# Products accumulated on a copied PSUM bank in the block scheme of two MLPs

## The chip, the core and the metric

One NeuronCore of a Trainium2 chip runs the whole program. TensorE (PE) multiplies and writes its sums to PSUM, which has eight banks of 128 partitions x 512 fp32 numbers here; ScalarE (ACT) and VectorE (DVE) read PSUM and SBUF; GpSimd (POOL) does little; SyncE (SP) issues the DMAs. The metric is the device time of the program in microseconds.

## What is computed

```
kv  = einsum(softmax(k over the sequence), v)        # 8 batches x 8 heads, 576 x 64
x   = softmax(q over the head's 64) @ kv             # joined to x [4608, 512]
h   = x @ moe_w_in;  g = h * sigmoid(1.702 h)        # [4608, 2048], layer 0
x   = g @ moe_w_out                                  # [4608, 512]
h   = x @ moe2_w_in; g = max(0.01 h, h)              # layer 1
out = g @ moe2_w_out
```

All in fp32. Every number that goes into a product is split into a high and a low half (`split_hi`, a cast on ScalarE; `split_lo`, a subtraction on VectorE), and every product is three matmul terms: high x high, low weight x high, high weight x low.

## The kernel before

The 4608 tokens are nine chunks of 512, which are columns of a matmul; the 512 features are four blocks of 128. Chunks 0 to 7 are taken in pairs (c, c + 1). A "pass" is one pair in one layer, written (layer, c): (0,0), (0,2), (0,4), (0,6), (1,0), (1,2), (1,4), (1,6), and chunk 8 apart. The attention of later chunks runs in the gaps of the layer-0 passes, step by step (maxima `kma`/`kmb`, exponentials, `kvp`, `kv` at L492, transposes `qtp`, the product `pxt` at L556).

The first matmul of a pair takes two blocks of the hidden dimension (columns f0, f1) and two chunks at a time, a "quad", with a scheme of seven block products in place of eight. Each product is six matmuls 128 x 512 (`product`, L732). A pass has eight quads. The seven products go to three PSUM banks, a, b and c (`ha`, `hb`, `hc`): the first to a, the second to b, the third to c, and then four more are accumulated on a, b, c, b. With p1 the first product, the four results are

- a after its second product,
- v5 = b (second product) + c's first + p1,
- u2 = b's first + p1 + c with its second product,
- p1 + b after its third product.

So the first product is copied to SBUF by ScalarE (L905), and VectorE makes five additions (the `add` at L900), each of which reads one bank and one tile of SBUF. The results go to the activation: `act1` (ScalarE, Tanh or Prelu) and in layer 0 `act2` (VectorE). In `quad_step` (passes (0,2), (0,4), (0,6), (1,0): 32 quads) the second matmul (`acc`, L789, 24 matmuls a quad) runs between the products. In `quad_apart` (passes (1,2), (1,4), (1,6): 24 quads) it doesn't; there `pair_apart` makes the second matmul behind it with the same seven-product scheme, in seven rounds of 24 matmuls on bank pairs a, c, a, b, b, c, b, and writes the results out through transposes (`out_part`: `otp`, then ScalarE's copy `ev`, then a store).

In layer 0, weights of layer 1 are prepared at the same time: raw blocks are loaded (`raw`), converted by ScalarE (L109, L112) and VectorE (L116 to L130), and stored again (`w`, `o`). PSUM is full: four banks `acc0` to `acc3`, three banks `h` (a, b, c) and one for the attention and the transposes.

What stands where on an engine is decided by a scheduler that goes through the program by priority; the code's own order and its `gaps` lists say where pieces of other work are offered. An engine then runs its instructions strictly in that order.

Of the kernel before, what the change touches and what calls it, by code (L numbers as in the profile page):

```python
# [26 lines left out]
def tile_softmax_linear_attention_two_mlps(  # L27
# [721 lines left out]
    def act1(layer, h, t):  # L749
        if layer == 0:  # L750
            nc.scalar.activation(t, h, AF.Tanh, scale=0.851)
        else:
            nc.scalar.activation(t, h, AF.Prelu, alpha=0.01)  # L753
# [135 lines left out]
    def run(items):  # L889
        for fn in items:  # L890
            fn()


    def quad_step(layer, n, gaps, extra):


        tiles = quad.pop((layer, n))
        W = {name: tiles[m][:, b, :, :] for name, (m, b) in OPS.items()}
        f0, f1 = 2 * n, 2 * n + 1
        add = lambda out, h, t: nc.vector.tensor_tensor(out=out, in0=h, in1=t, op=ALU.add)  # L900
        run(gaps[0])
        a = ps.tile([P, T], F32, tag="h", name="ha", bufs=3)
        product(a, "a11", W["w11"], True)
        p1 = pool["cv"].tile([P, T], F32, tag="p1", name="p1", bufs=2)
        nc.scalar.copy(p1, a)  # L905
        run(gaps[1])
        b = ps.tile([P, T], F32, tag="h", name="hb", bufs=3)
        product(b, "s2", W["t2"], True)
        u2 = pool["cv"].tile([P, T], F32, tag="u2", name="u2", bufs=2)
        add(u2, b, p1)  # L910
        run(gaps[2])
        c = ps.tile([P, T], F32, tag="h", name="hc", bufs=3)
        product(c, "s1", W["t1"], True)
        v5 = pool["cv"].tile([P, T], F32, tag="v5", name="v5", bufs=2)
        add(v5, c, p1)
        run(gaps[3])
        product(a, "a12", W["w21"], False)
        t11 = new_g(1, f0)
        act1(layer, a, t11)
        act2(layer, a, t11)  # L920
        halve_hi(f0, t11)
        run(gaps[4])
        product(b, "s3", W["t3"], False)
        add(v5, b, v5)
        halve_lo(f0)
        t22 = new_g(2, f1)
        act1(layer, v5, t22)
        act2(layer, v5, t22)
        run(gaps[5])
        product(c, "s4", W["w22"], False)  # L930
        add(u2, c, u2)
        run(gaps[6])
        t12 = new_g(1, f1)
        act1(layer, u2, t12)
        act2(layer, u2, t12)
        halve_hi(f1, t12)
        run(extra[0:1])
        halve_lo(f1)
        run(gaps[7])
        product(b, "a22", W["t4"], False)  # L940
        add(p1, b, p1)
        t21 = new_g(2, f0)
        act1(layer, p1, t21)
        run(gaps[8])
        act2(layer, p1, t21)
        run(extra[1:2])
        run(gaps[9])

# [2 lines left out]
    def quad_apart(layer, n, gaps):  # L951


        tiles = quad.pop((layer, n))
        W = {name: tiles[m][:, b, :, :] for name, (m, b) in OPS.items()}
        add = lambda out, h, t: nc.vector.tensor_tensor(out=out, in0=h, in1=t, op=ALU.add)  # L956
        m, o = divmod(n, 2)
        if o == 0:
            for name in ("a11", "a12", "a21", "a22"):
                G[name, m] = pool["g"].tile([P, 2, T], F32, tag=name, name=name, bufs=4)  # L960
        t11, t12, t21, t22 = (G[name, m][:, o, :] for name in ("a11", "a12", "a21", "a22"))
        run(gaps[0])
        a = ps.tile([P, T], F32, tag="h", name="ha", bufs=3)
        product(a, "a11", W["w11"], True)
        nc.scalar.copy(t21, a)
        run(gaps[1])
        b = ps.tile([P, T], F32, tag="h", name="hb", bufs=3)
        product(b, "s2", W["t2"], True)
        add(t12, b, t21)
        run(gaps[2])  # L970
        c = ps.tile([P, T], F32, tag="h", name="hc", bufs=3)
        product(c, "s1", W["t1"], True)
        add(t22, c, t21)
        run(gaps[3])
        product(a, "a12", W["w21"], False)
        act1(layer, a, t11)
        run(gaps[4])
        product(b, "s3", W["t3"], False)
        add(t22, b, t22)
        act1(layer, t22, t22)  # L980
        run(gaps[5])
        product(c, "s4", W["w22"], False)
        add(t12, c, t12)
        act1(layer, t12, t12)
        run(gaps[6])
        run(gaps[7])
        product(b, "a22", W["t4"], False)
        add(t21, b, t21)
        act1(layer, t21, t21)
        run(gaps[8])  # L990
        if o == 1:
            y = G["a21", m]
            nc.vector.tensor_tensor(out=y, in0=y, in1=G["a22", m], op=ALU.add)
        run(gaps[9])
# [15 lines left out]
    def pair_apart(c, steps, fetched):  # L1010


        add = lambda out, h, t: nc.vector.tensor_tensor(out=out, in0=h, in1=t, op=ALU.add)
        pages = [(r, m) for r in range(len(ROUNDS)) for m in range(NQ // 2)]
        halves_of = {}

        def prepare(k):
            r, m = pages[k]
            src = G[ROUNDS[r][1], m]
            hl = new_halves()  # L1020
            split_hi(src, hl[0])
            split_lo(src, *hl)
            halves_of[k] = hl
            if r == 0:
                sub(src, G["a21", m], src)
            elif r == 1:
                sub(src, G["a22", m], G["a11", m])
            elif r == 2:
                sub(src, src, G["a11", m])

        def acc2(n):
            tags = dict(a=("acc0", "acc1"), b=("acc2", "acc3"), c=("h", "h"))[n]
            return [ps.tile([P, T], F32, tag=t, name=f"o{n}", bufs=3 if t == "h" else 1) for t in tags]

        def tmp(tag):
            return [pool["cv"].tile([P, T], F32, tag=tag, name=tag, bufs=2) for _ in range(2)]

        banks = {}
        prepare(0)
        for k, (r, m) in enumerate(pages):  # L1040
            while len(fetched) < min(k + 4, len(pages)):
                rr, mm = pages[len(fetched)]
                fetched.append(load_round(ROUNDS[rr][0], mm))
            if k + 1 < len(pages):
                prepare(k + 1)
            run(steps.get(k, ()))
            name = "acabbcb"[r]
            if m == 0 and r in (0, 1, 3):
                banks[name] = acc2(name)
            w, (gh, gl) = fetched[k], halves_of.pop(k)  # L1050
            for l in range(2):
                for d in range(2):
                    sl = slice(d * P, (d + 1) * P)
                    for i, (wh, x) in enumerate(((0, gh), (1, gh), (0, gl))):
                        first_one = r in (0, 1, 3) and m == 0 and l == 0 and i == 0
                        nc.tensor.matmul(  # L1056
                            banks[name][d], w[:, l, wh, sl], x[:, l, :],
                            start=first_one, stop=(m == NQ // 2 - 1 and l == 1 and i == 2),
                            skip_group_check=(r not in (0, 1, 3)),
                        )  # L1060
            if m < NQ // 2 - 1:
                continue
            h = banks[name]
            for d in range(2):
                if r == 0:
                    if d == 0:
                        p1 = tmp("p1")
                    nc.scalar.copy(p1[d], h[d])
                elif r == 1:
                    if d == 0:  # L1070
                        v5 = tmp("v5")
                    add(v5[d], h[d], p1[d])
                elif r == 3:
                    if d == 0:
                        u2 = tmp("u2")
                    add(u2[d], h[d], p1[d])
                elif r == 2:
                    t = pool["cv"].tile([P, T], F32, tag="ev", name="ev", bufs=4)
                    nc.scalar.copy(t, h[d])
                    out_part(c, d, t)  # L1080
                elif r == 4:
                    add(v5[d], h[d], v5[d])
                    out_part(c + 1, 2 + d, v5[d])
                elif r == 5:
                    add(u2[d], h[d], u2[d])
                    out_part(c, 2 + d, u2[d])
                else:
                    add(p1[d], h[d], p1[d])
                    out_part(c + 1, d, p1[d])

    def pair_first(layer, c, units, held, work):

# [315 lines left out]

    ready(0)
    held = pair_second(0, 1, second_steps(units, (0, 2)))  # L1410
    for i, (layer, c) in enumerate(order):
        nxt = order[i + 1] if i + 1 < len(order) else None
        if split and c < LAST:
# [97 lines left out]
```

## Time and profile before

| | |
|---|---|
| median of 3 runs | 1627.37 us (1627.02 to 1627.89) |
| the profiled execution, whole | 1628.65 us |
| its span in the profile | 1626.9 us |
| PE busy | 1587.7 us, 98% |
| VectorE / ScalarE busy | 1053.7 / 800.9 us, 65% / 49% |
| granted TensorE clock, mean | 0.997 |

The profile is one execution. A timeline row gives the start, the duration, the engine and its line, output and input, and in brackets how long the engine stood idle before and what ended that. Matmuls in a row overlap, so the last one's duration reaches a little past the start of the next group. "PEld" is PE loading weights. The chain of waits is followed back from the last instruction to what released each step.

### The profile page before, as it was taken

What the parts mean: (1) busy time and instruction counts of PE and PEld (TensorE: products, weight loads), DVE (VectorE), ACT (ScalarE), POOL (GpSimd) and SP (SyncE); (2) the same over time, 40 slices, a digit from 0 to 9 for tenths busy, and PEclk for the clock granted to TensorE, in tenths of its full rate; (3) what the DMA queues carried; (4) which work ended last, traced back from release to release, by engine and by line L of the source; (5) the groups of instructions that cost most, each with busy time, mean ns of one, the idle gap of its engine ahead of it and who ended that gap; (6) DMA issues with size and microseconds to landing.
All of it is one profiled execution on the core that took longest, in us unless ns stands there. A gap on an engine that the chain in (4) does not pass through costs nothing.

```text
span 1626.9 us, 22121 instructions
## 1 busy us (share of the span) xinstructions
PE 1587.7 (98%) x7632; PEld 1268.3 (78%) x7632; DVE 1053.7 (65%) x1623; ACT 800.9 (49%) x1698; POOL 35.2 (2%) x162
## 2 busy tenths in 40 slices
PE   5999999999999999999999999999999999999998
PEld 3677778777877778778888888788888888888887
DVE  7899659786776757667544666644774487547411
ACT  7787656556545655445333545333453354334422
POOL 1000000000000002000000000000000000000000
PEclk9999999999999999999999999999999999999999
DMA  8788577778788887978896977996776777676763
GB/s 215 226 274 256 167 234 269 255 247 262 249 281 264 260 260 243 303 253 281 306 330 228 321 272 264 316 292 203 242 209 203 233 212 215 194 230 195 223 192 102
DMA packets 221775, 397.84 MB, mean 245 GB/s; under 512 B 57568, under 2 KB 138464, under 8 KB 221664
## 3 DMA queue, kind: packets, MB, share of 16 engines
q1 hardware_dynamic: 221664, 396.43, 76.1%
q8 instruction: 61, 1.00, 0.3%
q14 instruction: 50, 0.41, 0.1%
HBM read 306.18 MB, written 90.18 MB: 244 GB/s over the span
## 4 chain that ended last, share of the span: by engine, by line
PE 77%; DVE 7%; DMA 7%; issue 3%; ACT 1%; SPq 1%; ACTq 0%; DVEq 0%; POOL 0%; POOLq 0%
PE acc L789 23%; PE hb L732 13%; PE ha L732 9%; PE hc L732 8%; PE h L719 7%; PE ob L1056 6%; PE oa L1056 4%; PE oc L1056 4%; DMA o<-cv 2%; PE pxt L556 2%; DMA wo<-wp 1%; DMA w<-cv 1%; DVE cv L126 1%; DVE gl L86 1%; DMA raw<-in_moe_w_in_dram 1%
## 5 line engine op out<-in xcount | busy, mean ns | idle before, releaser
L789 PE MATMUL acc<-gh,wo 128*128 128x512 f32 x1152 | 362.8, 396 | 2.6 <-ACT wo L83 1.8
L789 PEld LDWEIGHTS acc<-gh,wo 128*128 128x128 f32 x1152 | 211.5, 188 | 48.9 <-ACT wo L83 2.2
L789 PE MATMUL acc<-gl,wo 128*128 128x512 f32 x576 | 225.6, 392 | 0.0
L719 PE MATMUL h<-x,wi 128*128 128x512 f32 x768 | 191.3, 399 | 2.8 <-ACT wi L83 2.8
L719 PEld LDWEIGHTS h<-x,wi 128*128 128x128 f32 x768 | 144.2, 191 | 37.2 <-ACT wi L83 4.4
L732 PE MATMUL ha<-x,wa 128*128 128x512 f32 x624 | 161.8, 393 | 2.8 <-ACT p L905 2.8
L732 PEld LDWEIGHTS ha<-x,wa 128*128 128x128 f32 x624 | 115.6, 188 | 33.0 <-issue 5.7
L83 ACT CAST sh<-a 128x1024 fp32r<-128x1024 f32 x84 | 88.2, 1050 | 94.4 <-PE oc L1056 35.1
L86 DVE TENSOR_TENSOR sl<-a,sh 128x1024 fp32r<-128x1024 f32 x84 | 102.7, 1222 | 49.4 <-ACT sh L83 49.0
L789 PEld LDWEIGHTS acc<-gl,wo 128*128 128x128 f32 x576 | 108.3, 188 | 23.8 <-issue 0.8
L956 DVE TENSOR_TENSOR a<-hb,a 128x512 f32<-128x512 f32 x72 | 49.7, 690 | 91.3 <-PE hb L732 91.3
L732 PE MATMUL hb<-x,wc 128*128 128x512 f32 x384 | 97.4, 389 | 0.0
L508 ACT ACTIVATE qt<-qt,qmx 128x64 f32<-128x64 f32 x256 | 86.0, 338 | 13.0 <-DVE qmx L498 12.2
L1056 PE MATMUL ob<-sh,wo 128*128 128x512 f32 x288 | 91.7, 394 | 0.0
L732 PE MATMUL hb<-xb,wb 128*128 128x512 f32 x336 | 86.1, 390 | 0.0
L83 ACT CAST gh<-gb 128x512 fp32r<-128x512 f32 x80 | 49.3, 617 | 71.8 <-PE acc L789 69.6
L732 PEld LDWEIGHTS hb<-x,wc 128*128 128x128 f32 x384 | 72.1, 188 | 14.9
L789 PE MATMUL acc<-wo,gh 128*128 128x512 f32 x256 | 79.2, 390 | 1.3 <-DMA wo<-wp 1.3
L83 ACT CAST gh<-gf 128x512 fp32r<-128x512 f32 x96 | 59.1, 616 | 42.5 <-DVE gf L757 33.6
L86 DVE TENSOR_TENSOR gl<-gb,gh 128x512 fp32r<-128x512 f32 x80 | 54.7, 687 | 35.5 <-ACT gh L83 34.2
L86 DVE TENSOR_TENSOR gl<-gf,gh 128x512 fp32r<-128x512 f32 x96 | 65.9, 687 | 18.0 <-ACT gh L83 17.1
L753 ACT ACTIVATE a<-a 128x512 f32<-128x512 f32 x72 | 45.5, 632 | 64.2 <-DVE a L956 64.2
(182 smaller groups left out, 2842.2 us busy)
## 6 DMA issues: line engine op xcount, KB each, us to landing
wo<-wo SPq DMA_DIRECT2D x144, 512.0 KB, 4.6
wo<-wp SPq DMA_DIRECT2D x68, 512.0 KB, 3.6
wo<-wt SPq DMA_DIRECT2D x48, 512.0 KB, 3.6
wa<-wq SPq DMA_DIRECT2D x40, 512.0 KB, 4.0
wb<-wq SPq DMA_DIRECT2D x40, 512.0 KB, 4.2
wc<-wq SPq DMA_DIRECT2D x40, 512.0 KB, 4.7
raw<-in_moe_w_in_dram SPq DMA_DIRECT2D x32, 512.0 KB, 4.9
raw<-in_moe_w_out_dram SPq DMA_DIRECT2D x32, 512.0 KB, 4.9
```

Of the source, the lines that this page charges most:

```text
L83: nc.scalar.copy(hi, src)
L86: nc.vector.tensor_tensor(out=lo, in0=src, in1=hi.bitcast(F32), op=ALU.subtract)
L126: nc.vector.scalar_tensor_tensor(out=w[:, o], in0=hw, scalar=0xC0000000, in1=w[:, o], op0=ALU.bitwise_and, op1=ALU.bitwise_or)
L508: nc.scalar.activation(t[:, h, r, :], t[:, h, r, :], AF.Exp, bias=mx[:, h, r : r + 1], accum_out=sm[:, h, r : r + 1],)
L556: nc.tensor.matmul(pv[o, :, a:e], kvb[b, j][o, :], t[o, :, a:e], start=True, stop=True)
L719: nc.tensor.matmul(h, WI[f][:, b, wh, o * P : (o + 1) * P], xs[f"a{side}{b + 1}"][xh][:, o, :], start=(i == 0), stop=(i == n - 1),)
L732: nc.tensor.matmul(h, w[:, wh, o * P : (o + 1) * P], xo[xh][:, o, :], start=(start and i == 0), stop=(i == 5), skip_group_check=not start,)
L753: nc.scalar.activation(t, h, AF.Prelu, alpha=0.01)
L789: nc.tensor.matmul(acc[d], lhsT, rhs, start=(f == 0 and i == 0), stop=(f == NF - 1 and i == 2))
L956: add = lambda out, h, t: nc.vector.tensor_tensor(out=out, in0=h, in1=t, op=ALU.add)
L1056: nc.tensor.matmul(banks[name][d], w[:, l, wh, sl], x[:, l, :], start=first_one, stop=(m == NQ // 2 - 1 and l == 1 and i == 2), skip_group ...
```

## The change

The first product's bank is no longer copied to SBUF but by ScalarE into the second bank, b. The products come in the order a, c, b, and b's product is accumulated upon the copy, so that p1 is inside bank b from then on. u2 and v5 start as ScalarE copies of b and c; two VectorE additions stay (v5 += b, u2 += c). The last result is bank b itself, which the activation reads from PSUM. The same is done in `quad_apart` and, with bank pairs, in `pair_apart`, where the last round's result is copied by ScalarE in place of an addition. Before the first quad three matmuls `hp` write the three `h` banks once. A quad has three ScalarE copies in place of one and two VectorE additions in place of five.

```diff
@@ quad_step
-        a = ps.tile([P, T], F32, tag="h", name="ha", bufs=3)
+        a, b, c = (ps.tile([P, T], F32, tag="h", name=f"h{x}", bufs=3) for x in "abc")
         product(a, "a11", W["w11"], True)
-        p1 = pool["cv"].tile([P, T], F32, tag="p1", name="p1", bufs=2)
-        nc.scalar.copy(p1, a)
+        nc.scalar.copy(b, a)
         run(gaps[1])
-        b = ps.tile([P, T], F32, tag="h", name="hb", bufs=3)
-        product(b, "s2", W["t2"], True)
-        u2 = pool["cv"].tile([P, T], F32, tag="u2", name="u2", bufs=2)
-        add(u2, b, p1)
-        run(gaps[2])
-        c = ps.tile([P, T], F32, tag="h", name="hc", bufs=3)
         product(c, "s1", W["t1"], True)
         v5 = pool["cv"].tile([P, T], F32, tag="v5", name="v5", bufs=2)
-        add(v5, c, p1)
+        nc.scalar.copy(v5, c)
+        run(gaps[2])
+        product(b, "s2", W["t2"], False)
+        u2 = pool["cv"].tile([P, T], F32, tag="u2", name="u2", bufs=2)
+        nc.scalar.copy(u2, b)
         run(gaps[3])
...
         product(b, "a22", W["t4"], False)
-        add(p1, b, p1)
         t21 = new_g(2, f0)
-        act1(layer, p1, t21)
+        act1(layer, b, t21)
         run(gaps[8])
-        act2(layer, p1, t21)
+        act2(layer, b, t21)
@@ quad_apart
         product(a, "a11", W["w11"], True)
-        nc.scalar.copy(t21, a)
+        nc.scalar.copy(b, a)
         run(gaps[1])
-        b = ps.tile([P, T], F32, tag="h", name="hb", bufs=3)
-        product(b, "s2", W["t2"], True)
-        add(t12, b, t21)
+        product(c, "s1", W["t1"], True)
+        nc.scalar.copy(t22, c)
         run(gaps[2])
-        c = ps.tile([P, T], F32, tag="h", name="hc", bufs=3)
-        product(c, "s1", W["t1"], True)
-        add(t22, c, t21)
+        product(b, "s2", W["t2"], False)
+        nc.scalar.copy(t12, b)
...
         product(b, "a22", W["t4"], False)
-        add(t21, b, t21)
-        act1(layer, t21, t21)
+        act1(layer, b, t21)
@@ pair_apart
             h = banks[name]
+            if r == 0:
+                banks["b"] = acc2("b")
+            elif r == 1:
+                v5 = tmp("v5")
+            elif r == 3:
+                u2 = tmp("u2")
             for d in range(2):
                 if r == 0:
-                    if d == 0:
-                        p1 = tmp("p1")
-                    nc.scalar.copy(p1[d], h[d])
+                    nc.scalar.copy(banks["b"][d], h[d])
                 elif r == 1:
-                    if d == 0:
-                        v5 = tmp("v5")
-                    add(v5[d], h[d], p1[d])
+                    nc.scalar.copy(v5[d], h[d])
                 elif r == 3:
-                    if d == 0:
-                        u2 = tmp("u2")
-                    add(u2[d], h[d], p1[d])
...
+                    nc.scalar.copy(u2[d], h[d])
...
                 else:
-                    add(p1[d], h[d], p1[d])
-                    out_part(c + 1, d, p1[d])
+                    t = pool["cv"].tile([P, T], F32, tag="ev", name="ev", bufs=4)
+                    nc.scalar.copy(t, h[d])
+                    out_part(c if r == 2 else c + 1, d, t)
@@ before the first quad
+    hi = XO["a11"][0]
+    for i in range(3):
+        h = ps.tile([P, T], F32, tag="h", name="hp", bufs=3)
+        nc.tensor.matmul(h, hi[:, 0, 0:P], hi[:, 0, :], start=True, stop=True)
```

The scheduler puts the instructions in another order. On ScalarE, at the head of the second quad of pass (0,4), before (`cv<-raw` are the two conversions, `gb<-p` the Tanh of the last quad's fourth result, `p<-ha` the copy of the first product):

```order
L83 CAST gh<-gf 128x512
L109 ACTIVATE cv_4790<-raw_4755 128x512
L112 ACTIVATE cv_4790<-raw_4755 128x512
L751 ACTIVATE gb<-p_4766 128x512
L905 COPY p_4911<-ha 128x512
L751 ACTIVATE gf<-ha 128x512
```

After, at the same place (`gb<-hb` is that Tanh, `hb<-ha` the copy into bank b, `v` and `u` the copies of c and b):

```order
L83 CAST gh<-gf 128x512
L751 ACTIVATE gb<-hb 128x512
L109 ACTIVATE cv_4779<-raw_4745 128x512
L112 ACTIVATE cv_4779<-raw_4745 128x512
L904 COPY hb<-ha 128x512
L908 COPY v_4915<-hc 128x512
L912 COPY u_4929<-hb 128x512
L751 ACTIVATE gf<-ha 128x512
```

The Tanh has moved ahead of the two conversions, and the copy stands right behind them.

On ScalarE, at the attention step of (0,4) around 545 us, before (L508 are the exponentials of q, `kv` the scaling of kvp, L587 the copy out of pxt):

```order
L751 ACTIVATE gf<-u_5305 128x512
L83 CAST gh<-gf 128x512
L109 ACTIVATE cv_5512<-raw_5377 128x512
L112 ACTIVATE cv_5512<-raw_5377 128x512
L751 ACTIVATE gb<-p_5289 128x512
L508 ACTIVATE qt,qsm<-qt,qmx 128x64
L492 ACTIVATE kv_5423<-kvp,krs 128x64
L508 ACTIVATE qt,qsm<-qt,qmx 128x64 x7
L587 COPY xr<-pxt 128x512
L905 COPY p_5479<-ha 128x512
```

After:

```order
L751 ACTIVATE gf<-u_5303 128x512
L83 CAST gh<-gf 128x512
L112 ACTIVATE cv_5493<-raw_5360 128x512
L751 ACTIVATE gb<-hb 128x512
L492 ACTIVATE kv_5405<-kvp,krs 128x64
L508 ACTIVATE qt,qsm<-qt,qmx 128x64 x6
L587 COPY xr<-pxt 128x512
L508 ACTIVATE qt,qsm<-qt,qmx 128x64 x2
L904 COPY hb<-ha 128x512
L908 COPY v_5477<-hc 128x512
L912 COPY u_5491<-hb 128x512
L109 ACTIVATE cv_5493<-raw_5360 128x512
```

The first conversion (L109) has moved from ahead of `kv` to behind the next quad's three copies; one exponential fewer stands ahead of `kv`.

On PE, at the end of the first pair's second matmul, before (`otp` are the four transposes of one page):

```order
L1056 MATMUL ob<-sl,wo 128x512
L732 MATMUL ha<-x,wa 128x512
L1004 MATMUL otp<-ident,p_10884 128x128 x4
L732 MATMUL ha<-x,wa 128x512 x3
L732 MATMUL hb<-xb,wb 128x512
L1004 MATMUL otp<-ident,p_10885 128x128 x4
L732 MATMUL hb<-xb,wb 128x512 x5
L732 MATMUL hc<-x,wb 128x512 x6
```

After:

```order
L1049 MATMUL ob<-sl,wo 128x512
L732 MATMUL ha<-x,wa 128x512
L997 MATMUL otp<-ident,ev 128x128 x4
L732 MATMUL ha<-x,wa 128x512
L732 MATMUL hc<-x,wb 128x512
L997 MATMUL otp<-ident,ev 128x128 x4
L732 MATMUL hc<-x,wb 128x512 x5
L732 MATMUL hb<-xb,wb 128x512 x6
```

Between the two groups of transposes stand two matmuls in place of four, and the product on c is ahead of that on b.

## Rows read from the trace of the kernel before

**Rows 1.** The page's parts 0 and 1: span, and busy time of each engine.

```profile
span 1626.9 us, 22121 instructions
...
PE 1587.7 (98%) x7632; PEld 1268.3 (78%) x7632; DVE 1053.7 (65%) x1623; ACT 800.9 (49%) x1698; POOL 35.2 (2%) x162
```

**Rows 2.** PE waits after 250 us: line, releaser: total us, times, longest.

```profile
PE pxt L556 <- ACT kv L492: 2.9, 3, 1.2
PE ha L732 <- ACT p L905: 2.8, 2, 2.4
...
PE hb L732 <- DVE u L900: 0.8, 1, 0.8
...
PE kmb L456 <- DVE km L451: 0.3, 1, 0.3
```

**Rows 3.** Chain that ended last, in pass (1,0): start, us, what.

```profile
917.82 2.72 PE acc L789 x12
...
932.78 2.72 PE acc L789 x12
```

**Rows 4.** Groups by form: count, busy us, mean ns, idle before.

```profile
L956 DVE TENSOR_TENSOR a<-hb,a 128x512 f32<-128x512 f32 x72 | 49.7, 690 | 91.3 <-PE hb L732 91.3
...
L900 DVE TENSOR_TENSOR p<-hb,p 128x512 f32<-128x512 f32 x32 | 21.9, 683 | 0.5 <-PE hb L732 0.5
...
L905 ACT COPY p<-ha 128x512 f32<-128x512 f32 x32 | 18.6, 581 | 12.3 <-PE ha L732 12.1
...
L965 ACT COPY a<-ha 128x512 f32<-128x512 f32 x24 | 14.1, 587 | 0.3
```

**Rows 5.** Timeline, a quad of pass (1,0): start, us, engine, line, idle before.

```profile
924.45 1.52 PE L732 MATMUL ha<-x,wa 128*128 128x512 f32 x6
...
926.01 0.59 ACT L905 COPY p<-ha 128x512 f32<-128x512 f32 x1 [0.74 <-PE ha L732]
...
927.17 1.52 PE L732 MATMUL hc<-xb,wb 128*128 128x512 f32 x6
...
929.89 1.52 PE L732 MATMUL hb<-x,wc 128*128 128x512 f32 x6
```

**Rows 6.** Timeline, head of the second quad of (0,4).

```profile
458.50 1.62 PE L732 MATMUL hc<-x,wb 128*128 128x512 f32 x6
...
460.85 0.65 ACT L112 ACTIVATE cv<-raw 128x512 f32<-128x512 f32 x1
...
462.54 1.66 PE L732 MATMUL ha<-x,wa 128*128 128x512 f32 x6 [2.42 <-ACT p L905]
...
466.39 1.53 PE L732 MATMUL hc<-xb,wd 128*128 128x512 f32 x6
```

**Rows 7.** Timeline, head of the second quad of (0,6).

```profile
652.03 1.22 PEld L732 LDWEIGHTS hc<-x,wb 128*128 128x128 f32 x6 [0.42 <-DVE p L900]
...
652.38 0.65 ACT L112 ACTIVATE cv<-raw 128x512 f32<-128x512 f32 x1
...
658.03 1.30 PE L732 MATMUL hc<-xb,wd 128*128 128x512 f32 x5
```

**Rows 8.** Timeline, one attention step inside (0,4).

```profile
545.52 0.67 ACT L109 ACTIVATE cv<-raw 128x512 uint32<-128x512 uint32 x1 [2.62 <-DMA wd<-wq]
...
550.75 1.08 PE L556 MATMUL pxt<-qT,kv 64*64 64x448 f32 x8 [1.19 <-ACT kv L492]
...
551.77 1.66 PE L732 MATMUL ha<-x,wa 128*128 128x512 f32 x6
...
554.39 0.57 ACT L905 COPY p<-ha 128x512 f32<-128x512 f32 x1
```

**Rows 9.** Timeline, end of the first pair's second matmul.

```profile
1221.01 1.37 DVE L1013 TENSOR_TENSOR p<-ob,p 128x512 f32<-128x512 f32 x2 [2.68 <-PE ob L1056]
...
1222.45 0.59 ACT L1006 COPY ev<-otp 128x512 f32<-128x512 f32 x1 [5.38 <-PE otp L1004]
...
1223.09 0.46 PEld L1004 LDWEIGHTS otp<-ident,p 128*128 128x128 f32 x4 [0.18 <-ACT ev L1006]
```

More of the change, by code (lines that the diff above doesn't have):

```diff
@@ L962, in quad_apart @@
         run(gaps[0])
-        a = ps.tile([P, T], F32, tag="h", name="ha", bufs=3)
+        a, b, c = (ps.tile([P, T], F32, tag="h", name=f"h{x}", bufs=3) for x in "abc")
         product(a, "a11", W["w11"], True)
-        nc.scalar.copy(t21, a)
+        nc.scalar.copy(b, a)
         run(gaps[1])
-        b = ps.tile([P, T], F32, tag="h", name="hb", bufs=3)
-        product(b, "s2", W["t2"], True)
-        add(t12, b, t21)
+        product(c, "s1", W["t1"], True)
+        nc.scalar.copy(t22, c)
         run(gaps[2])
-        c = ps.tile([P, T], F32, tag="h", name="hc", bufs=3)
-        product(c, "s1", W["t1"], True)
-        add(t22, c, t21)
+        product(b, "s2", W["t2"], False)
+        nc.scalar.copy(t12, b)
         run(gaps[3])
@@ L1047, in pair_apart @@
             name = "acabbcb"[r]
-            if m == 0 and r in (0, 1, 3):
+            if m == 0 and r < 2:
                 banks[name] = acc2(name)
@@ L1054, in pair_apart @@
                     for i, (wh, x) in enumerate(((0, gh), (1, gh), (0, gl))):
-                        first_one = r in (0, 1, 3) and m == 0 and l == 0 and i == 0
+                        first_one = r < 2 and m == 0 and l == 0 and i == 0
                         nc.tensor.matmul(
@@ L1058, in pair_apart @@
                             start=first_one, stop=(m == NQ // 2 - 1 and l == 1 and i == 2),
-                            skip_group_check=(r not in (0, 1, 3)),
+                            skip_group_check=(r >= 2),
                         )
@@ L1063, in pair_apart @@
             h = banks[name]
+            if r == 0:
[4 more added lines that the diff above has]
+                u2 = tmp("u2")
             for d in range(2):
                 if r == 0:
-                    if d == 0:
-                        p1 = tmp("p1")
-                    nc.scalar.copy(p1[d], h[d])
+                    nc.scalar.copy(banks["b"][d], h[d])
                 elif r == 1:
-                    if d == 0:
-                        v5 = tmp("v5")
-                    add(v5[d], h[d], p1[d])
+                    nc.scalar.copy(v5[d], h[d])
                 elif r == 3:
-                    if d == 0:
-                        u2 = tmp("u2")
-                    add(u2[d], h[d], p1[d])
[L1077 to L1080, printed above, removed]
+                    nc.scalar.copy(u2[d], h[d])
                 elif r == 4:
```

## The prediction

> **What bounds the kernel now.** The first thing to read is the page's busy table [rows 1]: TensorE (PE) is busy 1587.7 of 1626.9 us, 98%, VectorE (DVE) 65%, ScalarE (ACT) 49%. So the two engines between which the change moves work are not full, and a saved VectorE addition is worth nothing by itself. What counts is only (a) how many matmuls PE runs and (b) how long it stands between them.
>
> For (b) the view of PE's waits, cut to the stretch after 250 us where the changed code runs [rows 2]. The waits that lie in or beside changed code are pxt 2.9 us, ha 2.8, hb 0.8 and kmb 0.3, 6.8 us together: all that the change can win back. Everything else is pace. The chain of waits shows two places one quad apart in pass (1,0), 14.96 us apart [rows 3]; a row of 12 matmuls lasts 2.72 us there, 0.227 us each, and 66 matmuls (42 of the seven products, 24 of the second matmul) make 14.96. A steady quad has no hole.
>
> **The matmuls.** The product counts stay (7 x 6 in a quad). New are the three `hp` matmuls before the first quad: 3 x 0.227 = **+0.68 us** on PE. Nothing hides them, since nothing waits there on another engine for as long.
>
> **The additions that go.** 56 quads lose three additions each, of 683 to 690 ns, and gain two copies, of 581 to 587 ns [rows 4]. VectorE loses 56 x 3 x 0.69 = 116 us, ScalarE gains 56 x 2 x 0.585 = 66 us; the second matmul of the three pairs adds small change to both. Both engines stay under 70% of the span. On the path: 0, because the steady quads have no hole to fill.
>
> **The chain through bank b, steady quads.** This is the wait that the change adds. Before, product 1 is copied to SBUF, and its copy is needed only by VectorE. After, the copy writes bank b, and the third product, which accumulates into b, must wait for it on PE; everything behind it on PE waits too, as PE runs in order. The timeline of a quad gives the margin [rows 5]: product 1 starts at 924.45, its copy at 926.01 and takes 0.59, so it ends at 926.60; the third product starts at 927.17. With weights loaded 0.22 ahead of that the margin is 0.35 us at worst, 0.57 at best. The same again at the other end of b: the third product ends 1.36 + about 0.2 us after 927.17, the copy out to u2 runs from about 928.7 to 929.3, and bank b's next product starts at 929.89, margin 0.4 to 0.6. In the order of ScalarE's instructions the three copies stand directly behind each other in these quads, with nothing between. The unknown is how long a copy that *writes* PSUM takes: no row of before has ScalarE or VectorE writing PSUM. The nearest below is the copy that reads it, 0.58 us [rows 4]; above, an addition that reads a bank, 0.69, or a ScalarE instruction from SBUF to SBUF of the same width, 0.65 [rows 6]. All of 0.58 to 0.69 lies inside the margin: **0 us**, and I take 0.59.
>
> The Trainium skill speaks both ways here. "Perfetto Trace Analysis", Optimizing Tensor Performance, Matmuls, says that independent matmul groups should rotate through PSUM banks so that emptying one overlaps the next group's matmuls; the change ties a filling of b and an emptying of b between products, against that rule. By that rule the copy would show in each of the 56 quads, +33 us at 0.59 each; by the rows the product on the third bank in between covers it, 0.
>
> **Head of the second quad of (0,4).** Here there is a hole now. The copy of product 1 stands on ScalarE behind two conversions (L109, L112) that wait for a store, and behind a Tanh; PE waits 2.42 us for it before ha's next product [rows 6], and more by kmb and hb behind it. From 458.50 to 466.39 PE has 18 matmuls of the products, 4.08 us, and takes 7.89: 3.8 lost. After, the order on ScalarE is Tanh, L109, L112, copy: L112 ends at 460.85 + 0.65 = 461.50, the copy 0.57 later, so b (now third, due at 458.50) starts at about 462.1: 3.6 lost, and the later waits of this head are covered. **-0.2 us** (-1.2 if the conversions start earlier, +1.0 if the kmb and hb holes stay as well).
>
> **Head of the second quad of (0,6).** The same: from 652.03 to 658.03 PE has 18 matmuls, 4.08 us, and takes 6.0: 1.9 lost [rows 7], with the ha and hb waits of 0.38 and 0.81 in it. After, L112 is followed at once by the copy, which ends at 652.38 + 0.65 + 0.57 = 653.6; b is due at 651.9 to 652.0. 1.65 lost: **-0.25 us** (-1.2 to +0.8).
>
> **Attention steps in (0,4).** pxt waits for kv three times, 2.9 us in all [rows 2]. In the one shown [rows 8], L109 stands on ScalarE ahead of kv, with L112 behind it, and VectorE, which makes kv's factor, adds to p shortly before. In the new order of ScalarE L109 has moved behind the next quad's u2 copy, and the addition is gone. That is 0.67 + 0.68 [rows 4] less ahead of a wait of 1.19, which would end it; the other two share 1.7 us and may keep some: **-2.2 us** of the 2.9 (0 to -2.9). What stands ahead of kv next is L112 and one Tanh, which read what has long been there.
>
> **Copies delayed by the q exponentials in (0,4).** In the same stretch product 1 starts at 551.77 and its copy at 554.39, 2.62 later [rows 8], where the steady quad has 1.56 [rows 5]: 1.06 late, because ScalarE is in the middle of eight exponentials; in other quads of the pass it is less late. Before, this costs nothing: the copy is due with the fourth product. After, it is due with the third, 1.36 us earlier. Lateness beyond the margin of 0.35 to 0.57 shows: 0 to 0.25 in most of them, as an exponential moved ahead or behind shifts it. **+0.4 us** (0 to +1.2).
>
> **End of a pair's second matmul, three times.** Before, VectorE adds both pages to p from 1221.01 and PE transposes them (otp) between the first matmuls of the next quad: ScalarE's copy out of the first otp starts at 1222.45, the second otp's weights at 1223.09 [rows 9]. After, ScalarE has to copy both pages out of the banks and the first otp out too, in the order page, otp, page: the first from 1221.0, otp's at about 1222.3 and the second page's from 1222.9 to 1223.47, where the second otp can start, 0.38 later. And the order of PE has two matmuls between the transposes where four stood, so 2 x 0.227 us of cover is gone. 0.38 + 0.45 = 0.83 us, at two of the three pairs (at the third six matmuls stand there now): **+1.7 us** (+1.2 to +2.0). The seam from round 3 to 4 of each pair, where VectorE's addition becomes a ScalarE copy, has four matmuls of cover: 0 (0 to +0.5 each).
>
> **Sum**: 0.68 - 0.2 - 0.25 - 2.2 + 0.4 + 1.7 = **+0.13 us** on the span of 1626.9. The profiled execution took 1628.65 in all, 1.3 above the median 1627.37 of the runs; the difference carries over, so 1627.37 + 0.13 = **1627.5 us**. All the good ends together are 0.68 - 1.2 - 1.2 - 2.9 + 0 + 1.2 = -3.4; all the bad ends 0.68 + 1.0 + 0.8 + 0 + 1.2 + 2.0 + 1.5 = +7.2.
>
> **The rivals.** 0.2% of the time, 3.25 us, is about what a measurement of this kernel can tell from no change.
>
> *Slower: bank b's chain shows in every quad.* Place: the third product of 56 quads waits for the copy into PSUM, and product 5 (b's next) for the copy out. It decides once copy plus semaphore takes over 0.59 + 0.35 = 0.94 us, at either end. Each 0.1 us beyond costs 56 x 0.1 = 5.6 us at one end and 11 at both; a write to PSUM of 1.0 us would give about 1631, 1.1 us at both ends 1645. For it: no row shows such a write, and ScalarE gets 66 us more work, so a copy may also stand behind another instruction (0.6 us) in some quads. Against: all neighbouring rows lie under 0.7. The Trainium skill's "Perfetto Trace Analysis", Optimizing Scalar/DVE Operations, gives ScalarE a lower access overhead on PSUM (about 51 ns) than on SBUF (about 93 ns); by that the copy would be shorter than 0.59, and no row here shows it. I give this 0.10.
>
> *Slower: the small prices add up.* The order has changed all over the passes (0,4) and (0,6), where ScalarE is fullest, and where loads move on SP's queue. If the pxt waits stay (0 in place of -2.2) and the heads and the pair ends take their bad ends, the sum is +4 to +7: 1631.5 to 1634.5. 0.12.
>
> *Faster: the attention waits and the heads go altogether, and the pair's end is covered.* -3.3 or a bit more: 1623.5 to 1624. It needs nearly all the good ends at once. 0.08.
>
> *The change doesn't do what it says* (the additions gone, but nothing that PE was waiting for): that is, with other words, my forecast; a kernel whose sums went wrong would take the same time.
>
> **Chances and range.** Forecast (within 0.2%): 0.70, 1624.1 to 1630.6. Slower 0.22, faster 0.08. The range reaches from 1624.5, since the good ends can hardly meet all at once, to 1633, which takes in most of the second rival: about 0.8. The far end of the first rival is left out.
>
> **What would show it.** Right: a steady quad of (1,0) still 14.96 us; the copy into hb within 0.6 us, no PE wait on it outside (0,4) and (0,6); pxt waits at or under 1 us; one PE wait of 3 to 3.5 us before hb in the head of (0,4) and one near 1.6 in (0,6); otp waits at the pair ends of 0.4 us or more; VectorE's busy time lower by about 116 us. Wrong: quads longer than 14.96 or 9.52 us, PE waiting for the copy dozens of times, or DMA waits of PE that were not there before.

## The result

The changed kernel is slower: 1639.81 us median of four runs (1637.76 to 1641.29) against 1627.34 us (1627.02 to 1627.89) in the same rounds, a ratio of 1.0077 (95% interval 1.0065 to 1.0090). That is 12.5 us, nearly four times the 3.25 us (0.2%) that the prediction took as the limit of what can be told from no change, and outside its range.

The page of the changed kernel, parts 0 and 1 (for before see [rows 1]):

```profile
span 1637.7 us, 22064 instructions
...
PE 1593.5 (97%) x7635; PEld 1270.2 (78%) x7635; DVE 936.1 (57%) x1437; ACT 868.5 (53%) x1828; POOL 34.7 (2%) x162
```

VectorE has 117.6 us less and ScalarE 67.6 us more, as intended. The span is 10.8 us longer, and PE is *busy* for 5.8 us more, though it has only three matmuls more (0.7 us). The rest of that is matmuls that took longer. PE's waits after 250 us, to be held against [rows 2] (columns: line, what released it, total us, times, longest):

```profile
PE pxt L556 <- ACT kv L492: 4.0, 4, 2.7
PE acc L789 <- DMA wo<-wo: 2.6, 2, 1.7
PE ha L732 <- DMA wa<-wq: 2.5, 1, 2.5
PE otp L997 <- ACT ev L1078: 1.4, 2, 0.7
PE hb L732 <- ACT hb L904: 1.4, 3, 0.7
PE hb L732 <- ACT u L912: 0.8, 1, 0.8
```

Before, the wait for wo, which [rows 2] leaves out, was

```profile
PE acc L789 <- DMA wo<-wo: 0.7, 1, 0.7
```

The waits before ha on p, 2.8 us in [rows 2], are gone; the one of 0.8 us before hb on u is there as before, at another quad, and now on ScalarE's copy. pxt's waits have grown from 2.9 to 4.0, the longest of them from 1.2 to 2.7. The wait for wo has grown from 0.7 to 2.6, and those for wa and before the transposes (otp) are new. None of them is a wait of many quads: bank b's copy (hb <- hb) holds PE up three times in all.

The two longest waits are followed by slow matmuls. The first, in a timeline of all engines around 515 us (start, duration, engine, line, what, idle before and what ended it):

```profile
511.66 0.66 ACT L112 ACTIVATE cv<-raw 128x512 f32<-128x512 f32 x1 [3.94 <-DMA w<-cv]
...
513.75 0.15 DVE L489 TENSOR_SCALAR krs<-kvp 128x1 f32<-128x1 f32 x1
...
514.66 0.31 ACT L492 ACTIVATE kv<-kvp,krs 128x64 f32<-128x64 f32 x1 [1.87 <-DVE krs L490]
...
515.03 1.08 PE L556 MATMUL pxt<-qT,kv 64*64 64x384 f32 x8 [2.69 <-ACT kv L492]
...
516.04 2.88 PE L732 MATMUL ha<-x,wa 128*128 128x512 f32 x6
```

The conversion L112 stands on ScalarE ahead of the Tanh and kv. It waits 3.94 us for a store to land (w<-cv: the buffer that it will write), VectorE's work queues up behind it, krs (the factor of kv) is late, and PE stands for 2.69 us. The second, in PE's part of the timeline around 1083 us:

```profile
1083.19 2.90 PE L732 MATMUL ha<-x,wa 128*128 128x512 f32 x6 [2.55 <-DMA wa<-wq]
1085.88 1.68 PE L732 MATMUL hc<-x,wb 128*128 128x512 f32 x6
```

Six matmuls begin at 516.04 and at 1083.19 and last 2.88 and 2.90 us where six last 1.52 in a steady quad [rows 5]. The windows around both places say why (columns: window, its length, busy us and count of PE, PEld, DVE, ACT, POOL, then the granted clock, DMA share and GB/s):

```profile
512.00:515.00 3.00, 0.34 (x2) 0.00 (x0) 2.62 (x7) 1.11 (x3) 0.00 (x0) 1.00 0.80 192
516.00:519.00 3.00, 3.00 (x11) 2.27 (x9) 0.37 (x1) 2.47 (x14) 0.24 (x1) 0.52 0.90 324
...
1083.00:1086.00 3.00, 2.81 (x7) 2.26 (x8) 0.00 (x0) 0.00 (x0) 0.00 (x0) 0.50 1.02 393
1087.00:1090.00 3.00, 3.00 (x15) 2.47 (x14) 0.00 (x0) 1.17 (x2) 0.00 (x0) 1.00 0.42 127
```

In the first window PE is idle for 2.7 of 3 us; in the next one the granted clock is 0.52, then 0.50 behind the other wait: the lower of the engine's two levels, 1.2 GHz, for about three microseconds each time. Behind 516.04 PE has 13 matmuls' worth of work, 3.0 us at full pace, until hb at 520.84, and takes 4.8: 1.8 us lost. Behind 1083.19 two groups of six take 4.2 us in place of 2.7: 1.5 us lost. So the two places cost 2.69 + 1.8 and 2.55 + 1.5, **8.5 us**, where the span grew by 10.8. In the profile before, PE waited 0.54 us at the first place, too, so some 8 of the 8.5 are new. The rest is gains and losses of about 2 us and less; the largest loss among them is the wait for wo, 1.9 us more.

Where the second wait comes from is seen on SP. Before:

```profile
1063.51 0.32 SPq L294 DMA_DIRECT2D wa<-wq  x1
...
1066.59 0.52 SPq L285 DMA_DIRECT2D wt<-t  x1
1067.48 3.60 SPq L812 DMA_DIRECT2D out_dram<-ev  x4
```

After:

```profile
1072.04 0.52 SPq L285 DMA_DIRECT2D wt<-t  x1
1072.92 3.60 SPq L812 DMA_DIRECT2D out_dram<-ev  x4
1076.61 0.40 SPq L294 DMA_DIRECT2D wa<-wq  x1
```

wa, the weights of the second quad of pass (1,2), was issued ahead of the last six stores of the pass before it (two of weights, wt, of which one is shown, and four of the output); now it stands behind them, is issued 3.7 us after the four stores began, and PE gets to use it 6.6 us later.

And the steady quad of (1,0), for [rows 3] and [rows 5]:

```profile
921.14 1.52 PE L732 MATMUL hb<-x,wc 128*128 128x512 f32 x6
...
931.99 0.57 ACT L904 COPY hb<-ha 128x512 f32<-128x512 f32 x1 [0.74 <-PE ha L732]
...
933.38 1.52 PE L732 MATMUL hb<-xb,wb 128*128 128x512 f32 x6
...
936.10 1.52 PE L732 MATMUL hb<-x,wc 128*128 128x512 f32 x6
```

From hb at 921.14 to hb at 936.10 is 14.96 us, unchanged. The copy into bank b ends at 932.56, and the product that accumulates on it starts at 933.38. ScalarE's copy that writes PSUM, by form:

```profile
L904 ACT COPY hb<-ha 128x512 f32<-128x512 f32 x32 | 18.4, 574 | 17.7 <-PE ha L732 17.7
```

574 ns, where the copy that writes SBUF took 581 [rows 4]. "Perfetto Trace Analysis" of the Trainium skill, Optimizing Scalar/DVE Operations, has a smaller access overhead for ScalarE on PSUM than on SBUF; the direction agrees, the gain here is 7 ns (13 against the 587 of the other copy in [rows 4]).

### The profile page after: what moved, and what is told of

Same layout as the page of the kernel before. It is cut to its first block, busy times and chain, and to the rows that moved or that the text cites. A ratio compares the mean times of both kernels' runs of the same rounds, so it can differ in the third digit from the quotient of the medians.

```text
span 1637.7 us, 22064 instructions
## 1 busy us (share of the span) xinstructions
PE 1593.5 (97%) x7635; PEld 1270.2 (78%) x7635; DVE 936.1 (57%) x1437; ACT 868.5 (53%) x1828; POOL 34.7 (2%) x162
## 5 line engine op out<-in xcount | busy, mean ns | idle before, releaser
L952 DVE TENSOR_TENSOR a<-hb,a 128x512 f32<-128x512 f32 x24 | 16.6, 692 | 157.7 <-PE hb L732 157.7
L508 ACT ACTIVATE qt<-qt,qmx 128x64 f32<-128x64 f32 x256 | 86.2, 340 | 12.5 <-DVE qmx L498 12.5
L732 PE MATMUL hc<-x,wb 128*128 128x512 f32 x288 | 75.7, 396 | 0.5 <-DVE gb L757 0.5
```

The source lines that it names most:

```text
L508: nc.scalar.activation(t[:, h, r, :], t[:, h, r, :], AF.Exp, bias=mx[:, h, r : r + 1], accum_out=sm[:, h, r : r + 1],)
L732: nc.tensor.matmul(h, w[:, wh, o * P : (o + 1) * P], xo[xh][:, o, :], start=(start and i == 0), stop=(i == 5), skip_group_check=not start,)
```

## The experiments

The theory after reading the trace: two waits moved by the new order, each with a stretch of half clock behind it, and the pair ends. The rival: the chain through bank b costs a little in each of the 56 quads, and the two waits are accidents of the one execution that was profiled. Ratios are to the kernel before, measured in the same rounds. Single executions of one kernel differ by some us (29 of the kernel before, in the rounds of three of these runs, lie between 1621.9 and 1631.7), so a profile shows which waits one execution had, and the medians what an edit is worth.

**The wa load earlier.** In the changed kernel, the loads wb and wa of the second quad of (1,2) are asked for at the end of the second matmul before; the order of SP then has wa ahead of the stores, and nothing else changes place but one wb load.

```diff
                 spread(steps, sum_pieces(range(SUMS, NQ)), 0)
+                spread(steps, [lambda: load_quad(1, 1, 1), lambda: load_quad(1, 1, 0)], 12, 0)
...
-                    gaps[1].append(lambda: load_quad(layer, m, 1))
-                    gaps[4].append(lambda: load_quad(layer, m, 0))
+                    if (layer, c, n) != (1, 2, 0):
+                        gaps[1].append(lambda: load_quad(layer, m, 1))
+                        gaps[4].append(lambda: load_quad(layer, m, 0))
```

> The changed kernel with the two loads wb and wa for the second quad of pass (1,2) asked for earlier in the program, so that wa is issued on SP ahead of two wt stores and four output stores; nothing else moves. Theory (two displaced waits with a clock drop behind each): PE's 2.55 us wait before ha and the matmuls at half clock behind it (about 1.7 us) go, so about 4.2 us less than the changed kernel: 1635.6, and the granted clock of that stretch is 1.0. Rival (bank b's chain through ScalarE costs a little in every quad): no change, 1639.8.

Measured: 1635.55 us, ratio 1.0048 (1.0032 to 1.0064). PE's waits after 250 us no longer hold one for wa:

```profile
PE pxt L556 <- ACT kv L492: 2.4, 3, 1.2
PE acc L789 <- DMA wo<-wo: 2.1, 1, 2.1
```

The granted clock between 1070 and 1100 us is 1.00. 4.3 us gone, as forecast, by moving one load. The chain through bank b, which this leaves alone, can't have been that part of the loss. All profiles below agree: wherever wa stands ahead of the stores, PE waits 0.2 us for it at most; in the three with wa behind them (the changed kernel twice, and the next run) it waits 2.55, 3.4 and 4.1 us, each time with half clock behind it.

**L112 kept behind L109.** The second conversion gets the same pin as the first.

```diff
             tc.keep_in_program_order(i)
-        nc.scalar.activation(w.bitcast(F32), hw.bitcast(F32), AF.Abs)
+        i = nc.scalar.activation(w.bitcast(F32), hw.bitcast(F32), AF.Abs)
+        if pin:
+            tc.keep_in_program_order(i)
```

> The changed kernel with the second conversion (L112) kept behind the first on ScalarE, so that it no longer stands ahead of kv, where it waits for a store. Theory: the pxt waits of 4.0 us after 250 us fall under 1 us, the stretch of half clock behind the 2.69 us wait goes too (1.7 us): 4 to 5 us less than the changed kernel, about 1635.3. Rival (bank b's chain): 1639.8. A third outcome, that the wait for the store moves to the next instruction that needs ScalarE, would leave PE waits of 2 us or more elsewhere in (0,4) and a time of 1638 or more.

Measured: 1634.69 us, ratio 1.0045 (1.0028 to 1.0062). No wait before pxt is left among PE's waits:

```profile
PE ha L734 <- DMA wa<-wq: 4.1, 1, 4.1
PE hb L734 <- ACT hb L906: 2.8, 3, 1.3
```

The late wa is still there, in this execution with 4.1 us, and the copy into hb holds PE up for 2.8 us at the heads of quads. The price of L112's place is 5 us by the medians, and the wait for the store did not turn up elsewhere at that size. All profiles say the same of the stretch that holds the three pxt waits of before, from the start of the third quad of (0,4) to that of the seventh (first matmul to first matmul): 74.65 us before (76.1 in another execution of the same code there), 71.6 to 72.3 in the five kernels with L112 kept behind L109 in the quads, 73.5 to 76.9 in the six profiles with the change in `quad_step` and without that.

**Both.** The two edits above together. The run also holds the last wt stores behind that wa load on SP; the order of SP is the same in "All mended" below, which has no such line.

> Both edits together (the earlier wa load, and L112 kept behind L109). Theory: the savings add, 8 to 9 us less than the changed kernel: about 1631, 3 to 4 us above the kernel before, which would be the pair ends, hp and DMA waits of PE around 780 to 806 us. Rival (bank b's chain): 1639.8.

Measured: 1632.02 us, ratio 1.0028 (1.0016 to 1.0040): 7.8 us less than the changed kernel, so the savings add but for 1.6 us, and the ratios' intervals are as wide as that. Left on PE, among others (the otp waits are still 1.4 us):

```profile
PE acc L796 <- DMA wo<-wo: 3.0, 1, 3.0
...
PE ha L739 <- DMA wa<-wq: 0.2, 1, 0.2
```

**The copy into b made twice** in the 32 quads of `quad_step`, to measure the margin of bank b's chain.

```diff
         nc.scalar.copy(b, a)
+        nc.scalar.copy(b, a)
```

> The changed kernel with the copy of bank a into bank b made twice in quad_step (32 quads), which lengthens the chain through bank b by one copy, 0.57 us, and measures its margin. Theory (the margin is 0.35 to 0.57 us, so one copy is free or nearly): 0 to 0.22 us in each of 32 quads, 0 to 7 us more than the changed kernel. Rival (the chain is already exposed in every quad): 0.57 us in each, 18 us more, 1658.

Measured: 1640.03 us, ratio 1.0079 (1.0061 to 1.0097), 0.2 us above the changed kernel. A quad of (1,0), and SP's queue, where the four stores of the output begin at 1080.05:

```profile
923.23 0.57 ACT L904 COPY hb<-ha 128x512 f32<-128x512 f32 x1 [0.25 <-PE ha L732]
...
923.83 0.57 ACT L905 COPY hb<-ha 128x512 f32<-128x512 f32 x1
...
924.62 1.52 PE L732 MATMUL hb<-xb,wb 128*128 128x512 f32 x6
...
1075.95 0.32 SPq L294 DMA_DIRECT2D wa<-wq  x1
```

The second copy ends at 924.40, and the accumulating product starts at 924.62, at its time. The margin of the chain is more than a whole copy in the steady quads. But the 0.2 us aren't the price of the copies: with them the scheduler has put wa ahead of the stores again, and PE doesn't wait for it. The kernel to compare with is the one with the earlier wa load, 1635.55 us in the same rounds, and against it the copies cost 4.5 us. They are seen at heads of quads in (0,4) and (0,6), where that kernel has two waits for bank b, 0.7 us together, and this one

```profile
PE hb L732 <- ACT hb L905: 6.1, 5, 2.1
```

The rival, which asked for 18 us more, falls here.

**One half of the change at a time.** First `quad_step` alone (with hp), `quad_apart` and `pair_apart` as before.

> The change in quad_step alone (32 quads, with hp), while quad_apart and pair_apart stay as before. In the order of SP, wa for the second quad of (1,2) stands ahead of the stores again. Theory: the changed kernel less the late wa (4.2 us) and the two pair ends (1.4): 1634.2, with PE's wait before pxt of about 2.7 us and the half clock behind it still there. Rival (bank b's chain shared by all 56 quads): 32/56 of the 12.5 us, 1634.4 as well, but then without that wait and that clock dip in the trace.

Measured: 1634.76 us, ratio 1.0044 (1.0031 to 1.0058). The median is the one forecast, but the rival's 1634.4 is as near, and the trace was to tell them apart. The profiled execution took 1630.2, and it has neither a long pxt wait nor a clock drop there (its one drop, 0.83 in the 10 us from 770, is behind a wait for wo):

```profile
PE acc L789 <- DMA wo<-wo: 3.6, 2, 2.4
PE pxt L556 <- ACT kv L492: 2.1, 4, 0.6
```

So this run doesn't decide between the two; what excludes the rival is the copy made twice. The other half, `quad_apart` and `pair_apart` alone, without hp:

> The change in quad_apart and pair_apart alone (24 quads and three pairs), quad_step as before, no hp matmuls. Theory: only the pair ends cost, two PE waits of 0.7 us: 1.4 us above the kernel before, about 1628.6, and no late wa. Rival (bank b's chain): 24/56 of 12.5 us, 1632.7.

Measured: 1628.08 us, ratio 1.0008 (0.9998 to 1.0019).

```profile
PE otp L1001 <- ACT ev L1082: 1.4, 2, 0.7
PE acc L789 <- DMA wo<-wo: 0.8, 2, 0.6
```

The pair ends are there with two waits of 0.7, and no wait for wa. PE's longer waits lie in code that is as before: the profiled execution was the slowest of its twelve, 1633.12 us, with 1.91 us before ha and 2.1 before pxt in (0,4), and a granted clock of 0.83 in the 10 us from 460 and from 500. So a long pxt wait with half clock behind it can come without the change. In both halves wa is issued ahead of the stores; only the two together push it behind. So 12.5 us is not the sum of the halves (7.2 and 1.3 by their ratios): some 4 us of it comes from an order that neither half has, as much as the earlier wa load gave.

**A second look at `quad_step` alone**, whose executions spread from 1629.0 to 1637.0.

> A second look at the change in quad_step alone, whose twelve executions spread from 1629.0 to 1637.0 with a gap between 1632.6 and 1633.5, and whose first profile fell among the fast ones. Theory (L112 ahead of kv waits for a store whose landing varies, and a long wait brings the half clock with it): if this execution takes over 1633, its trace has a pxt wait above 2 us in (0,4) and a stretch of lower granted clock behind it; if it takes less, pxt waits stay under 1 us. Rival: the slower executions are slower for another reason (DMA waits of PE near 775 and 802 us), with pxt waits under 1 us in either.

Measured: 1628.07 us, a single execution, its waits:

```profile
PE acc L789 <- DMA wo<-wo: 3.5, 2, 2.1
PE pxt L556 <- ACT kv L492: 1.5, 2, 1.3
```

pxt waits 1.3 us at most, above the "under 1" that was forecast, and the DMA waits are as long as in the execution profiled before. What the executions above 1633 us wait for was not caught in a profile, and stays open.

**A second look at the changed kernel.**

> A second look at the changed kernel as it is. Theory: the wait of PE for wa at the second quad of (1,2) is there again at 2 to 4 us, as it comes from the order of SP; the pxt wait near 515 us may be smaller or larger, as it hangs on when a store lands; time 1637 to 1641. Rival (both long waits were accidents of one execution): neither is above 1 us, and the time is still 1637 or more.

Measured: 1637.38 us. wa is late again, by more, with slow matmuls behind it:

```profile
1080.88 2.65 PE L732 MATMUL ha<-x,wa 128*128 128x512 f32 x6 [3.42 <-DMA wa<-wq]
```

pxt waits 1.6 us at most this time, with no clock drop, and the wo loads near 775 and 802 us hold PE up for 4.1 us in place of 2.6. The wait for wa belongs to the order; how long the one behind L112 is changes from execution to execution, as it hangs on when a store lands.

**All mended.** Both edits, and in the last round of `pair_apart` VectorE copies the banks out.

```diff
-                    nc.scalar.copy(t, h[d])
+                    (nc.scalar.copy if r == 2 else nc.vector.tensor_copy)(t, h[d])
```

> The changed kernel with the earlier wa load, L112 kept behind L109, and the last round's two copies out of the banks made by VectorE in place of ScalarE. Theory: the otp waits of 1.4 us at two pair ends go, so 1.4 us less than the version with the first two edits (1632.0): 1630.6. Rival (the pair's end is bound by PE's order, with two matmuls between the transposes): no change, 1632.0, and the otp waits stay, now behind VectorE.

Measured: 1629.81 us, ratio 1.0017 (1.0006 to 1.0028), 2.2 us less than with the two edits; by the ratios, from different rounds, it is 1.8, with intervals as wide as that, so the time alone doesn't show the gain. The trace does: no otp wait is left. What is:

```profile
PE acc L791 <- DMA wo<-wo: 2.1, 2, 1.2
PE hb L734 <- ACT hb L906: 1.7, 3, 0.9
```

The pair's end was ScalarE's queue, not PE's order. The mended kernel is still some 2.8 us above the kernel before.

**Two attempts to get below it.** Both keep the edits of "All mended", with L112 pinned in the quads only; the second also moves the conversions in the second matmul of a layer-0 pass one or two groups earlier (places 0, 2, 5, 7, 9, 11 in place of 0, 3, 6, 9, 11, 13).

> All mended, but L112 kept behind L109 only for the conversions that run in the quads, not for those in the second matmul of a pass. Theory: the wait of 1.2 us at 802 us behind L112 goes and the heads keep their waits of about 1.7: 1628.8. Rival (L112 moves in front of kv or a cast again somewhere): 1630 or more.

> As the one before, and the conversion steps in the second matmul of a layer-0 pass start one or two groups earlier (places 0, 2, 5, 7, 9, 11 in place of 0, 3, 6, 9, 11, 13), so that the last one is over before the next pass begins. Theory: the copy into bank b at the second quads of (0,4) and (0,6) no longer stands behind conversions that wait for a store, so PE's waits before hb and hc there (2.6 us) go: 1626.5, about the kernel before. Rival (the denser DMA traffic makes the weights late): DMA waits of PE grow by as much, 1629 or more.

Measured: 1635.19 us, ratio 1.0054 (1.0038 to 1.0071), and 1635.56 us, ratio 1.0051 (1.0034 to 1.0068). Both miss by 6 to 9 us, in part for the same kind of reason at another place. The first of them, around 608 us (timeline as above, PE and ScalarE), and its wait for wo:

```profile
607.40 0.35 ACT L510 ACTIVATE qt<-qt,qmx 128x64 f32<-128x64 f32 x1 [4.02 <-DVE qmx L500]
...
608.09 1.51 PE L558 MATMUL pxt<-qT,kv 64*64 64x448 f32 x8 [2.88 <-ACT kv L494]
...
779.57 1.19 PE L791 MATMUL acc<-gh,wo 128*128 128x512 f32 x2 [2.38 <-DMA wo<-wo]
```

kv stands on ScalarE behind the first exponential of q (L510 here), which waited for its maximum, and PE waits 2.88 us for kv. In the other kernel it is 2.36 us at the same place:

```profile
606.84 1.08 PE L558 MATMUL pxt<-qT,kv 64*64 64x448 f32 x8 [2.36 <-ACT kv L494]
...
776.18 1.19 PE L791 MATMUL acc<-gh,wo 128*128 128x512 f32 x2 [2.40 <-DMA wo<-wo]
```

The waits for wo have half clock behind them in both (granted 0.87 in the 10 us from 780, and 0.83 in those from 770). From the start of the last quad of (0,6) to that of the first of (1,0) both take 152.7 to 152.8 us, where "All mended" takes 148.6: in the profiles, that is as large a part of the miss as kv, or larger.

No version here beats the kernel before.

## Why the prediction was wrong

*What bounds the kernel, and that the saved additions are worth nothing*: right. VectorE's 117.6 us less (116 forecast) bought nothing.

*Bank b's chain, 0 us*: right for the steady quads, 14.96 us each with 0.574 us a copy, and there a second copy is free. At heads of quads the chain does show, 1.4 us in all. The first rival, to which 0.10 went, is the one that the experiments exclude.

*The heads of (0,4) and (0,6), -0.45 us*: wrong in form, and the sum is near by luck. One wait of 3.5 us and one of 1.6 were forecast; in the two quads treated, bank b's waits are 0.43 and 0.22. The quad in (0,4) takes 2.0 us less than before: it begins 2.3 us later, while L109, which waits for a store, starts at 460.54 where it started at 460.29; the one in (0,6) takes 1.0 less. Two quads that the prediction doesn't treat take 2.3 us more together: the first of (0,4), with a wait of 0.73 for bank b, and the third of (0,6), with 0.76 for u.

*Attention steps, -2.2 us*: **the step that failed first.** The prediction took off L109's 0.67 us and the addition's 0.68, as work that had moved from ahead of kv, and went on: "What stands ahead of kv next is L112 and one Tanh, which read what has long been there." It asked what L112 reads and not what it writes. The row that it rested on [rows 8] had the answer in its bracket: L109 had waited 2.62 us for a DMA before it ran (the bracket names a load; elsewhere in that trace L109 waits for the stores of the same buffers, w<-cv and o<-cv, 19 times, and L112 3 times). The first of the two to write the buffer carries the wait; with L109 moved away, L112 is the first (13 such waits in the changed kernel, none with L112 kept behind), and it still stands ahead of kv. In place of -2.2 the pxt waits took 1.1 us more in the profile, and 1.8 went in half clock; how much, changes from execution to execution. Keeping L112 behind L109 gave 5 us back, and with it the stretch of those steps is 2.4 to 3.1 us shorter than before, near the 2.2 forecast: the size was right for an order that the scheduler didn't make.

*The order of SP*: **the step that was missing.** The prediction names loads that move on SP's queue in (0,4) and (0,6), in a rival's sentence, and prices none; the load that mattered most stands at the seam from (1,0) to (1,2), in code that the diff doesn't touch. It cost 2.55 + 1.5 us, and putting it back gave 4.3. The prediction's own list of what would show it wrong ends with "DMA waits of PE that were not there before"; that sign came.

*Half clock*: no term had it, since the one long wait in the trace of before, 2.42 us [rows 6], has none behind it. It is a matter of the execution, too: the second half of the change alone has two such stretches in code as before.

*Pair ends, +1.7 us*: right in place, with 1.4 us of waits (0.70 twice). A row of it:

```profile
1232.97 0.59 ACT L1078 COPY ev<-ob 128x512 f32<-128x512 f32 x1
...
1233.62 0.66 PE L997 MATMUL otp<-ident,ev 128*128 128x128 f32 x4 [0.70 <-ACT ev L1078]
```

*The q exponentials, +0.4, and hp, +0.68*: not told apart from the rest. *The second rival* (small prices add up in (0,4), (0,6) and on SP) had the right places, with 1631.5 to 1634.5 and a chance of 0.12; its price left out the clock and the seam.

What is left of the mended kernel's 2.8 us: hp, and PE's waits for wo near 775 and 802 us, 0.7 us in before, 0.8 with the second half of the change alone, and 1.4 to 4.1 (their row acc <- wo<-wo) in each kernel with the change in `quad_step`. Four of these eleven profiles have half clock behind such a wait. From the start of the last quad of (0,6) to that of the first of (1,0), the stretch takes 146.7 us before, 146.9 with the second half alone and 148.6 to 152.8 with `quad_step` changed: 2 to 6 us, a third price of the change that the prediction didn't have and no edit here removed. On SP one of the wo loads there stands, in the changed kernel, behind a fourth store of x where it stood ahead of it. That this is the cause was argued from the order and not tried.

## What to carry to other kernels

An instruction that moves takes its wait along, or leaves it to the next one that writes the same buffer: price a move by the bracket of idle time before the row, not by the row's duration. When a scheduler sets the order, go through every load that moves later on the DMA queue over the whole program and ask who needs it when, above all at seams between passes that the diff doesn't touch; one load behind six stores cost 4.1 us here, more than all the prediction's good ends together (3.4). A copy into a PSUM bank that later products accumulate on cost PE nothing here in the steady quads, where a product of six matmuls stood between, but it saved nothing either, since VectorE wasn't the bound. And when a run changes one line, look whether the scheduler has moved something else before reading its time: the copy made twice seemed free only because a load had moved back.

## What the runs showed of the hardware

Half clock after a wait: granted 0.50 for about three microseconds behind PE waits of 2.55 and 2.69 us, 1.5 to 1.8 us lost each. "Perfetto Trace Analysis" of the Trainium skill, Matmul Optimizations, says that the matmul engine scales its power by its use, so that matmuls should come back to back; the rows agree. The wait's length alone doesn't decide it: 2.42 us [rows 6], the 2.36 us above and the 3.0 us for wo in "Both" left the pace at full, while in the second half of the change alone a wait of 1.91 us was followed by six matmuls in 2.24 us:

```profile
465.22 2.24 PE L732 MATMUL ha<-x,wa 128*128 128x512 f32 x6 [1.91 <-ACT p L905]
```

The 10 us from 460 have a granted clock of 0.83 there. What decides it is open.
